# Second group's keys in a buffer of their own, loaded early; sixth and later weight loads held by a one-element write

## The chip, the cores and the metric

The kernel runs on one core of a Trainium2 chip. The metric is the device time of one execution in microseconds (us); lower is better. Five engines work side by side, each with its own instruction stream: TensorE (PE; PEld is its weight load), VectorE (DVE), ScalarE (ACT), GpSimd (POOL) and SyncE (SP, which here only issues DMAs). They wait for each other by semaphores. A DMA issued on SP fetches from main memory into a tile.

## The reference

Three stages, all in float32:

```python
# delta-rule attention: B=4, H=8, S=768, D=48
k_n = k / (norm(k, axis=-1) + 1e-06)
for t in range(S):
    y[:, :, t] = einsum('bhd,bhde->bhe', q[:, :, t], state)
    v_old = einsum('bhde,bhd->bhe', state, k_n[:, :, t])
    state = state + beta[t] * einsum('bhd,bhe->bhde', k_n[:, :, t], v[:, :, t] - v_old)
x = y.transpose(0, 2, 1, 3).reshape(3072, 384)
g = x @ w_gate; x = (silu(g) * (x @ w_val)) @ w_out   # w: 384x1536, 384x1536, 1536x384
h = x @ w_in;   out = elu(h) @ w_out2                 # w: 384x2048, 2048x384
```

## The kernel before

The 3072 tokens are worked in twelve groups of 256: two batches by 128 sequence steps. Group `g` passes through `prepare` (norms of the keys, transposes of queries and keys, Gram matrices, L447 to L604), `invert` (a triangular inverse by 32 small DVE steps, L642 to L724) and `attention` (X, the matrices G, the chain of states, the outputs, their transposes, L746 to L895). Then `moe1(g)` applies the first pair of projections and `w_out` for twelve slices of the hidden width, each with three passes of high and low parts, so that float32 precision comes out of a faster matrix format. Its result goes to memory. After all groups `moe2` does the second pair.

The weights arrive as 64-bit patterns and are decoded on the chip. One weight tile `w0` ... `w17` holds a pair of slices; `load_w` issues its DMAs (L931, L934), and `decode` turns it into high and low parts in about six instructions on ACT (L954, L960, L965, L982) and DVE (L968, L972, L986). Slices `f` = 0, 1 of `moe1` need tiles 0 to 2, slices 2, 3 need 3 to 5, and so on. So the first 130 us hold the attention of groups 0 and 1, the decoding of eighteen tiles and the first slices of `moe1(0)`, all on DVE and ACT.

The order of the instructions on every engine is fixed ahead of the run by a planner (`Order.run`, L134 on): each step names the engines it can run on, estimated costs, a priority, and what it reads and writes, and the planner picks the next one. Where it expects PE to be idle it puts in matmuls whose result nobody reads (`fill`, L1217; `fill2`, L1228). It also keeps count of PE's instructions in blocks of 256 (`fetch`, L104 on).

Names that the change and the prediction touch: `kp` and `qp` are the tiles of keys and queries, shared by all groups; the zero columns of `kp` are set in `c1` (L394). `loads(g, ...)` issues the DMAs of keys, queries and values. `norm` inside `prepare` squares the keys (L477 on DVE or POOL, L481 on ACT), sums (L485), takes the root (L489) and inverts (L493, L495); `nkn` (L536) scales the keys; `rk` (L541) and `kb` (L546) copy them on. The X step is L772 on PE and its copies into `gr` are L777; the G step is L792 in four sets per group, and its copies are L801. `gr` is also written by `kb`, so that POOL's `kb` of group 1 waits until group 0 has read it. `load_w` of tile 5 and later carries `mark[PAUSE]`, the last X copy of group 0, as a predecessor in the planner alone: no semaphore stands behind it.

Of the kernel before, what the change touches and what calls it, by code (L numbers as in the profile page):

```python
# [245 lines left out]
def delta_moe_kernel(ctx: ExitStack, tc: tile.TileContext, q, k, v, beta,  # L246
# [15 lines left out]
    UNTIL = 170e3  # L262
    JOIN = (4,)
    AHEAD = 5
    PAUSE = (0, 'x')
    HOLD = (0, 'm')
    WARM = 8
    P1 = 14.7
# [25 lines left out]
    low = zd[:, 1:2]  # L294
    nbt = T("nbt", [128, NI, B * H])

    kp = T("kp", [128, 16, 64])
    qp = T("qp", [128, 16, 64])
    R = T("R", [128, 16, 96])
    kq = T("kq", [128, 2, 4, 2, 128])  # L300
# [81 lines left out]
    def consts():  # L382
        def c0():
            make_identity(nc, ident)
            G.memset(strict, 1.0)
            for r in range(4):
                s = strict[32 * r:32 * r + 32, :]
                G.affine_select(out=s, in_=s, compare_op=ALU.is_ge, fill=0.0, base=-1,
                                pattern=[[1, 32]], channel_multiplier=-1)
        add(0, [("POOL", 2500.0, 2500.0, 0, c0)], w=["ident", "strict"])  # L390

        def c1():
            V.memset(neg1, -1.0)
            V.memset(kp[:, :, D:64], 0.0)  # L394
            V.memset(qp[:, :, D:64], 0.0)
        add(0, dve(600, c1, 3), w=["neg1", "kpz", "qpz"])

        def c2():
            for r in range(4):
                q0 = slice(32 * r, 32 * r + 32)  # L400
                V.tensor_copy(eye[q0], ident[q0, q0])
            V.tensor_reduce(out=low, in_=ident.rearrange("p (r h m) -> p h r m", r=4, h=2)[:, 1],
                            op=ALU.add, axis=AX.XY)
            V.tensor_scalar(out=zd[:, 0:1], in0=low, scalar1=-1.0, scalar2=1.0,
                            op0=ALU.mult, op1=ALU.add)
        add(20, dve(220, c2, 6), r=["ident"], w=["eye", "zd"])
# [35 lines left out]

    SHIFT = ((0, 0, 128, 0), (4, 0, 64, 64), (4, 64, 128, 0))

    def loads(g, p, then=None, after=()):
        for a0, a1 in ((0, 1), (1, 2)) if g == 0 else ((0, 2),):
            add(p, dma(196608 * (a1 - a0), lambda a0=a0, a1=a1: nc.sync.dma_start(  # L447
                out=kp[:, a0 * 8:a1 * 8, 0:D], in_=src_of(k, g, a0, a1)), 160.0),
                w=[("k", x) for x in range(a0, a1)], after=after)
        if then:  # L450
            then()
        for a0, a1 in ((0, 1), (1, 2)) if g == 0 else ((0, 2),):
            add(p, dma(196608 * (a1 - a0), lambda a0=a0, a1=a1: nc.sync.dma_start(
                out=qp[:, a0 * 8:a1 * 8, 0:D], in_=src_of(q, g, a0, a1)), 160.0),
                w=[("q", x) for x in range(a0, a1)], after=after)
        for a in range(2):
            def rv(a=a):
                x = src_of(v, g, a, a + 1)
                for u0, p0, p1, m0 in SHIFT:
                    nc.sync.dma_start(out=R[p0:p1, a * 8 + u0:a * 8 + u0 + 4, D:2 * D],  # L460
                                      in_=x[m0:m0 + p1 - p0, u0:u0 + 4])
            add(p, [("SP", 1290.0, 0.0, 196608 / 160.0, rv)], w=[("Rv", a)])

    ALLA = [("ain", n) for n in range(4)]

    def prepare(g, p):
        i, b0 = ax_of(g)
        ss, s, r = sm
        sq = ain[:, 0:768].rearrange("p (u d) -> p u d", d=D)
        two = g == 0  # L470

        def norm(u0, u1, keys):
            u = slice(u0, u1)
            n = D * (u1 - u0)

            def square(e):
                return lambda: e.tensor_tensor(out=sq[:, u], in0=kp[:, u, 0:D], in1=kp[:, u, 0:D],  # L477
                                               op=ALU.mult)

            def squared():  # L480
                A.activation(out=sq[:, u], in_=kp[:, u, 0:D], func=ACTF.Square)  # L481
            part = [("sq", x) for x in keys]
            add(p, dve(n, square(V)) + (act(n, squared, False) if two else pool(n, square(G))),
                r=[("k", x) for x in keys] + ([] if u0 else ALLA[:3]), w=part + ([] if u0 else ALLA[:3]))
            add(p, dve(n, lambda: V.tensor_reduce(out=ss[:, u], in_=sq[:, u], op=ALU.add, axis=AX.X)),  # L485
                r=part + ALLA[:3], w=[("ss", x) for x in keys])

            if g < 2:
                add(p, act(u1 - u0, lambda: A.activation(out=r[:, u], in_=ss[:, u], func=ACTF.Sqrt), False),  # L489
                    r=[("ss", x) for x in keys] + ["sqrt"], w=[("sm", x) for x in keys])  # L490

                def over():
                    V.tensor_scalar(out=r[:, u], in0=r[:, u], scalar1=-1.0, scalar2=-1e-6, op0=ALU.mult,  # L493
                                    op1=ALU.add)
                    V.reciprocal(out=s[:, u], in_=r[:, u])  # L495
                add(p, [("DVE", 400.0, 490.0, 0, over)], w=[("sm", x) for x in keys])
                return
            sk = [("sm", x) for x in keys]

            def guess():  # L500
                V.tensor_scalar(out=s.bitcast(I32), in0=ss.bitcast(I32), scalar1=-0.5,
                                scalar2=float(0x5f3759df), op0=ALU.mult, op1=ALU.add)
            add(p, [("DVE", 100.0, 180.0, 0, guess)], r=[("ss", x) for x in keys], w=sk)
            for _ in range(3):
                def newton():
                    V.scalar_tensor_tensor(out=r, in0=s, scalar=-0.5, in1=ss, op0=ALU.mult, op1=ALU.mult)
                    V.tensor_tensor(out=r, in0=r, in1=s, op=ALU.mult)
                    V.scalar_tensor_tensor(out=s, in0=r, scalar=1.5, in1=s, op0=ALU.add, op1=ALU.mult)
                add(p, [("DVE", 430.0, 510.0, 0, newton)], w=sk)

            def over():
                V.tensor_tensor(out=r, in0=ss, in1=s, op=ALU.mult)
                V.tensor_scalar(out=r, in0=r, scalar1=-1.0, scalar2=-1e-6, op0=ALU.mult, op1=ALU.add)
                V.reciprocal(out=s, in_=r)
            add(p, [("DVE", 500.0, 590.0, 0, over)], w=sk)
# [33 lines left out]
        def trans(a, which):  # L549
# [13 lines left out]
            def rest():  # L563
                add(p, act(512, part(A.copy)) + (dve(512, part(V.tensor_copy)) if two else []),
                    r=[h], w=[("kq", a, which)], use=[h])
            return (436, f, ["ident", n + "z", ("qk"[which], a)], h,
                    [("kq", a, which)], rest)
        batch(p, 2, [trans(0, 0), trans(1, 0)], g > 0)
        for a in range(2):
            add(p, dve(384, lambda a=a: nkn(a)), r=[("sm", a)], w=[("k", a)])  # L570
        if two:
            add(p, dve(512, mb), r=["strict", "nbt"], w=zk, need=[hm])
        batch(p, 2, [trans(0, 1), trans(1, 1)], g > 0)
        later = []
        for a in range(2):
            def scaled(a=a, after=()):
                add(p, (dve if two else pool)(384, lambda: kb(a)), r=["nbt", ("k", a)], w=[("grk", a)],
                    wait=GX[a], after=after)
            if not two:
                scaled()  # L580
            else:
                later.append(scaled)
            for n, c in enumerate(SHIFT):
                add(p + 0.9, act(192, lambda a=a, c=c: rk(a, *c), False), r=[("k", a)],
                    w=[("Rk", a, n)])
        for a in range(2):
            l = []
# [330 lines left out]
    opened = {}  # L918

    sent = []  # L920

    def load_w(n, srcs, p, after=()):
        def f():
            if srcs[0][0].dtype == I32:
                buf[n] = TT(f"w{n}", [128, 2, 2 * DM], I32)
            else:
                buf[n] = TT(f"w{n}", [128, 2, DM])
            for j, (src, cols) in enumerate(srcs):
                rv = buf[n][:, j]
                if not cols:  # L930
                    nc.sync.dma_start(out=rv, in_=src)  # L931
                    continue
                rv = rv.rearrange("p (kk f) -> p kk f", kk=KD)
                nc.sync.dma_start(out=rv, in_=src.rearrange("(kk p) f -> p kk f", p=128))  # L934
# [296 lines left out]
    def warm():  # L1231
        fill(WARM)
        od.fill = fill
        od.quick = quick
    loads(0, 0, betas)
    consts()
    add(0, [("ACT", 1400.0, 1500.0, 0, lambda: A.activation(
        out=sm[2][:, 0:1], in_=neg1, func=ACTF.Sqrt, scale=-1.0))], r=["neg1"], w=["sqrt"])
    add(0, act(128, lambda: A.copy(out=identr, in_=ident), False), r=["ident"], w=["identr"])
    add(0, pe(230 * WARM, warm, 1, 2 * WARM), r=["identr"])  # L1240
    beta_rows()
    prepare(0, att_pri(0))
    rows()
    attention(0, att_pri(0) + 1)

    def new_dt():
        buf['dt'] = TT("dt", [128, 2, 2, DM], I32)
    add(0, [("SP", 1.0, 0.0, 0.0, new_dt)], w=[("dt", 0), ("dt", 1)])
    for n in range(NW):
        load_w(n, src1(n), 1 + n, [] if n < AHEAD else [mark[PAUSE], sent[n - 2]])  # L1250
        tag, tk = (("xh1", ["xh1"]), (0, [("dt", 0)]), ("xl1", ["xl1"]), (1, [("dt", 1)]))[
# [1 line left out]
        decode(n, tag, tk, att_pri(0) + 4.8 + 0.02 * n)  # L1253
    for g in range(NB):
        if g:
            loads(g, 100 + 10 * g if g > 1 else PL1, None, [sent[NW - 1]] if g == 2 else [])
            prepare(g, att_pri(g) - 5 if g > 1 else P1)
            attention(g, att_pri(g) + 1 if g > 1 else P1)
        moe1(g, MP + 100 * g)
# [54 lines left out]
```

## Time and profile before

| | us |
|---|---|
| median of 3 runs (1142.50 to 1144.47) | 1144.07 |
| the profiled execution | 1148.89 |
| span of its trace | 1147.2 |
| PE busy in the span | 1116.3 |
| DVE busy | 808.2 |
| ACT busy | 562.0 |

The profiled execution took 1.69 us around its span and 4.82 us more than the median. The rows below are of this one execution; "idle before" in square brackets is the time in which the engine had nothing to run just before the instruction, with what ended it.

### The profile page before, as it was taken

The numbers are of one execution on the slowest core, as the hardware profiler recorded it, in microseconds if no ns is written. First come the engines' busy times: TensorE is split into PE (matmuls) and PEld (weight loads), VectorE is DVE, ScalarE is ACT, GpSimd is POOL, SyncE is SP. The second block draws the span as 40 slices with busy tenths as digits, with TensorE's granted clock in tenths as the row PEclk, the third lists the DMA queues.
The fourth block names the chain that finished last, engine by engine and source line by source line (L and its number), as shares of the span: only waits on it lengthen the run. The fifth ranks groups of instructions, "written<-read, shape, count | busy, mean of one in ns | idle before, by whom it ended". The sixth has DMA issues, their size and how long they took to land.

```text
span 1147.2 us, 34358 instructions
## 1 busy us (share of the span) xinstructions
PE 1116.3 (97%) x14711; PEld 1027.4 (90%) x14711; DVE 808.2 (70%) x2489; ACT 562.0 (49%) x1104; POOL 43.3 (4%) x57
## 2 busy tenths in 40 slices
PE   8899999999999999999999999999999999999998
PEld 6688989999899899899999999988888888898887
DVE  7889877877888777878787775995545444454444
ACT  7798442424343424243424234995545454454444
POOL 0100010100010100000001000000000000000000
PEclk9899999999999999899999899999999999999999
DMA  8770211020202120202020005900101001010000
GB/s 197 212 205 17 44 31 30 16 44 9 51 17 44 25 35 9 51 9 51 9 51 10 22 3 170 344 2 28 55 1 55 1 14 42 1 37 1 28 1 28
DMA packets 107625, 57.36 MB, mean 50 GB/s; under 512 B 77744, under 2 KB 102320, under 8 KB 107472
## 3 DMA queue, kind: packets, MB, share of 16 engines
q1 hardware_dynamic: 107472, 55.16, 18.3%
q8 instruction: 115, 1.88, 0.7%
q14 instruction: 38, 0.31, 0.1%
HBM read 45.71 MB, written 9.44 MB: 48 GB/s over the span
## 4 chain that ended last, share of the span: by engine, by line
PE 86%; DVE 8%; ACT 4%; issue 2%; DVEq 0%; ACTq 0%
PE gv L1028 26%; PE acc L1054 12%; PE acc L1180 9%; PE at L1180 9%; PE gv L1143 9%; PE at L1143 8%; PE at L792 3%; PE at L828 3%; PE at L557 2%; PE at L772 2%; PE at L598 2%; PE at L862 1%; PE acc L1217 1%; DVE sv L834 1%; ACT tb L1035 1%
## 5 line engine op out<-in xcount | busy, mean ns | idle before, releaser
L1028 PE MATMUL gv<-xh,w 128*128 128x256 f32 x1728 | 291.3, 288 | 1.4 <-ACT tb L1035 0.9
L1028 PEld LDWEIGHTS gv<-xh,w 128*128 128x128 f32 x1728 | 241.3, 193 | 7.2 <-ACT tb L1035 2.3
L1054 PE MATMUL acc<-hb,w 128*128 128x256 f32 x1296 | 183.6, 287 | 0.5 <-ACT hb L1042 0.5
L1054 PEld LDWEIGHTS acc<-hb,w 128*128 128x128 f32 x1296 | 165.7, 192 | 6.3 <-issue 2.4
L1035 ACT ACTIVATE tb<-gv 128x256 f32<-128x256 f32 x144 | 55.5, 385 | 226.5 <-PE gv L1028 225.9
L1028 PE MATMUL gv<-xl,w 128*128 128x256 f32 x864 | 151.8, 284 | 2.8 <-issue 2.0
L1028 PEld LDWEIGHTS gv<-xl,w 128*128 128x128 f32 x864 | 125.1, 193 | 3.3 <-issue 2.3
L1038 DVE TENSOR_TENSOR tb<-gv,tb 128x256 f32<-128x256 f32 x144 | 60.3, 419 | 62.2 <-ACT tb L1035 42.9
L1042 ACT CAST hb<-tb 128x256 fp32r<-128x256 f32 x144 | 58.7, 407 | 89.3 <-DVE tb L1038 89.3
L1158 DVE SCALAR_TENSOR_TENSOR hb<-gv,hb 128x512 f32<-128x512 f32 x48 | 33.2, 691 | 92.0 <-ACT hb L1155 92.0
L657 DVE TENSOR_TENSOR ain<-z,ain 128x60 f32<-128x60 f32 (+32 forms) x522 | 89.0, 209 | 2.4
L664 DVE TENSOR_TENSOR z<-z,ain 128x60 f32<-128x60 f32 (+32 forms) x522 | 89.2, 210 | 1.0
L1158 DVE SCALAR_TENSOR_TENSOR hb<-at,hb 128x512 f32<-128x512 f32 x48 | 33.2, 691 | 79.6 <-ACT hb L1155 79.4
L1149 ACT ACTIVATE hb<-gv 128x512 f32<-128x512 f32 x48 | 28.8, 599 | 94.5 <-PE gv L1143 94.3
L1045 DVE TENSOR_TENSOR hb<-tb,hb 128x256 fp32r<-128x256 f32 x144 | 63.2, 439 | 14.4 <-ACT hb L1042 12.8
L1155 ACT ACTIVATE hb<-hb,neg 128x512 f32<-128x512 f32 x96 | 69.7, 726 | 3.0
L1149 ACT ACTIVATE hb<-at 128x512 f32<-128x512 f32 x48 | 28.7, 598 | 78.4 <-PE at L1143 78.1
L1152 ACT ACTIVATE hb<-hb 128x512 f32<-128x512 f32 x96 | 60.9, 634 | 2.9
L792 PE MATMUL at<-gr,R 32*96 32x80 f32 x1480 | 47.9, 255 | 1.5 <-issue 1.5
L792 PEld LDWEIGHTS at<-gr,R 32*96 32x96 f32 x1480 | 39.9, 162 | 8.6 <-issue 2.7
L1143 PE MATMUL gv<-lc,w 128*128 128x512 f32 x144 | 41.2, 394 | 0.0
L1143 PE MATMUL at<-lc,w 128*128 128x512 f32 x144 | 40.9, 394 | 0.0
(212 smaller groups left out, 2080.9 us busy)
## 6 DMA issues: line engine op xcount, KB each, us to landing
w<-in_moe_w_out_dram SPq DMA_DIRECT2D x28, 384.0 KB, 7.1
w<-in_moe_w_in_dram SPq DMA_DIRECT2D x16, 384.0 KB, 6.3
w<-in_moe_w_gate_dram SPq DMA_DIRECT2D x12, 384.0 KB, 8.1
w<-in_moe_w_val_dram SPq DMA_DIRECT2D x12, 384.0 KB, 7.7
qp<-in_q_dram SPq DMA_DIRECT2D x11, 384.0 KB, 6.2
kp<-in_k_dram SPq DMA_DIRECT2D x11, 384.0 KB, 4.6
x2d<-hb SPq DMA_DIRECT2D x12, 256.0 KB, 2.0
R<-in_v_dram SPq DMA_DIRECT2D x24, 96.0 KB, 2.2
```

The source lines that it names most:

```text
L657: V.tensor_tensor(out=t, in0=z[:, l:l + 1, x:y].to_broadcast([128, m, y - x]), in1=an[:, l + 1:32, l:l + 1].to_broadcast([128, m, y - x]), ...
L664: V.tensor_tensor(out=z[:, l + 1:32, x:y], in0=z[:, l + 1:32, x:y], in1=t, op=ALU.add)
L792: PE.matmul(bank[h[c].got[0]][0:96, s * 80:s * 80 + 80], lhsT=R[t, u, :], rhs=gr[t, u, 0:80], start=True, stop=True, skip_group_check=True)
L1028: PE.matmul(dst, lhsT=wt[:, a_, kk * 128:(kk + 1) * 128], rhs=xx[:, kk, :], start=(n == 0), stop=(n == 3 * KD - 1))
L1035: A.activation(out=c['s'], in_=bank[h.got[0]][:, 0:TB], func=ACTF.Silu)
L1045: return lambda: e.tensor_tensor(out=c['h'][:, 1, :], in0=c['s'], in1=c['h'][:, 0, :].bitcast(F32), op=ALU.subtract)
L1054: PE.matmul(o_, lhsT=w[:, a_, d * 128:(d + 1) * 128], rhs=c['h'][:, b_, :], start=(f == 0 and n == 0 and d != 1), stop=(f == F1 - 1 and n ...
L1143: PE.matmul(x, lhsT=W[f][:, 0, a_, kk * 128:(kk + 1) * 128], rhs=x2[n][b_][:, kk, :], start=(m == 0), stop=(m == 3 * KD - 1))
L1152: A.activation(out=c['r'], in_=c['r'], func=ACTF.Exp, scale=-1.0)
L1155: A.activation(out=c['r'], in_=c['r'], func=ACTF.Identity, bias=neg1, scale=1.0)
L1158: V.scalar_tensor_tensor(out=c['r'], in0=bank[h.got[0]], scalar=0.0, in1=c['r'], op0=ALU.max, op1=ALU.add)
L1180: PE.matmul(o, lhsT=c['h'][:, b_, t * 128:(t + 1) * 128], rhs=W[f][:, 1][:, a_, :], start=(f == 0 and m == 0), stop=(f == F2 - 1 and m == 2))
```

## The change

Group 1's keys get a tile of their own, `kpx[1]` (tag `l2`), with its zero columns set on POOL. `loads` is split: `load_k(1)` and `norms(1)` are added to the planner's list ahead of the attention of group 0, the queries and values of group 1 behind it. For group 1 the squares go to a scratch tile `xh0` instead of `ain`, and may be made on DVE or ACT instead of DVE or POOL. `PAUSE` now names a new step, `gate`: it allocates the tile of weight 5 and lets ACT copy one element of `gr`, where X has just been written, into it. The DMAs into that tile must wait for that write, and all DMAs behind them on SP with them.

```diff
-    PAUSE = (0, 'x')
+    PAUSE = 'gate'
...
-    kp = T("kp", [128, 16, 64])
+    kpx = [T("kp", [128, 16, 64]), T("l2", [128, 16, 64])]
...
+        add(0, pool(256, lambda: G.memset(kpx[1][:, :, D:64], 0.0)), w=["l2"])
...
-    def loads(g, p, then=None, after=()):
+    def kkey(g, a):
+        return "l2" if g == 1 else ("k", a)
+
+    def load_k(g, p, after=()):
+        kp = kpx[g == 1]
...
+    def load_qv(g, p, after=()):
...
-    def prepare(g, p):
-        i, b0 = ax_of(g)
+    def norms(g, p):
         ss, s, r = sm
-        sq = ain[:, 0:768].rearrange("p (u d) -> p u d", d=D)
+        kp = kpx[g == 1]
+        sqs = {0: ain[:, 0:768].rearrange("p (u d) -> p u d", d=D)}
+        sk_ = ["xh0"] if g == 1 else ALLA[:3]
...
+            def scratch():
+                if g == 1:
+                    sqs[0] = TT("xh0", [128, 16, D])
+                return sqs[0][:, u]
...
-            add(p, dve(n, square(V)) + (act(n, squared, False) if two else pool(n, square(G))),
+            add(p, dve(n, square(V)) + (act(n, squared, False) if g < 2 else pool(n, square(G))),
...
+    held = set()
...
         def f():
-            if srcs[0][0].dtype == I32:
+            if n in held:
+                held.discard(n)
+            elif srcs[0][0].dtype == I32:
                 buf[n] = TT(f"w{n}", [128, 2, 2 * DM], I32)
...
-    loads(0, 0, betas)
+    load_k(0, 0)
+    betas()
+    load_qv(0, 0)
...
+    norms(0, att_pri(0))
     prepare(0, att_pri(0))
     rows()
+    load_k(1, PL1)
+    norms(1, P1)
     attention(0, att_pri(0) + 1)
+    load_qv(1, PL1)
...
+    def gate():
+        n = AHEAD
+        held.add(n)
+        buf[n] = TT(f"w{n}", [128, 2, 2 * DM], I32) if src1(n)[0][0].dtype == I32 else TT(f"w{n}", [128, 2, DM])
+        A.copy(out=buf[n].bitcast(F32)[0:1, 0, 0:1], in_=gr[0:1, 0, 0:1])
+    mark['gate'] = add(att_pri(0) + 1, act(1, gate, False), r=[("gx", 0, 0)], w=[f"w{AHEAD}", f"w{AHEAD}b"])
...
-            loads(g, 100 + 10 * g if g > 1 else PL1, None, [sent[NW - 1]] if g == 2 else [])
+            if g > 1:
+                load_k(g, 100 + 10 * g, [sent[NW - 1]] if g == 2 else [])
+                norms(g, att_pri(g) - 5)
+                load_qv(g, 100 + 10 * g, [sent[NW - 1]] if g == 2 else [])
```

The planner's order moves with it. On SP, the queue of DMAs, the keys of group 1 stood behind weight 4 and in front of weight 5. Before (the names `w5_20_634` and so on begin with the weight tile's number):

```order
L453 DMA qp_70<-in_q_dram 128x16x48 [waits DMAHW3_49,PE_49]
L934 DMA w4_9_212<-in_moe_w_gate_dram 128x3x256 [waits DMAHW4_49]
L934 DMA w4_9_212<-in_moe_w_val_dram 128x3x256 [waits DMAHW5_49]
L447 DMA kp_69<-in_k_dram 128x16x48 [waits DVE_49,DMAHW6_49,PE_49,Activation_49]
L931 DMA w5_20_634<-in_moe_w_out_dram 128x768 [waits DMAHW7_49]
L931 DMA w5_20_634<-in_moe_w_out_dram 128x768 [waits DMAHW0_49]
```

The same stretch of SP's queue now:

```order
L452 DMA l2_70<-in_k_dram 128x16x48 [waits DMAHW7_49]
L951 DMA w2_7_177<-in_moe_w_out_dram 128x768 [waits DMAHW0_49]
L951 DMA w2_7_177<-in_moe_w_out_dram 128x768 [waits DMAHW1_49]
L954 DMA w3_8_188<-in_moe_w_gate_dram 128x3x256 [waits DMAHW2_49]
L954 DMA w3_8_188<-in_moe_w_val_dram 128x3x256 [waits DMAHW3_49]
L458 DMA qp_71<-in_q_dram 128x16x48 [waits DMAHW4_49,PE_49]
L954 DMA w4_9_233<-in_moe_w_gate_dram 128x3x256 [waits DMAHW5_49]
L954 DMA w4_9_233<-in_moe_w_val_dram 128x3x256 [waits DMAHW6_49]
L951 DMA w5_16_581<-in_moe_w_out_dram 128x768 [waits DMAHW7_49,Activation_49]
```

The keys moved in front of weight 2 and wait for no engine; weight 5 waits for ACT. On ACT, around the second half of the inverse (L724 before, L741 now), the rows before were:

```order
L724 COPY ain_74<-at3_88 128x256
L982 CAST w0_13_525<-xh1_10_289 128x2x384
L982 CAST w1_14_528<-dt_3_138 128x2x384
L954 ACTIVATE w4_9_212<-w4_9_212 128x768
L960 ACTIVATE xh1_15_532<-w4_9_212 128x768
L724 COPY ain_74<-at0_85 128x256
L777 COPY gr_73<-at1_86 128x4x80
```

and they are now:

```order
L741 COPY ain_75<-at3_89 128x256
L501 ACTIVATE sm2_80<-sm0_78 128x16
L1002 CAST w0_14_532<-xh1_10_292 128x2x384
L974 ACTIVATE w4_9_233<-w4_9_233 128x768
L985 ACTIVATE w2_7_177<-w2_7_177 128x768
L741 COPY ain_75<-at0_86 128x256
L1280 COPY w5_16_581<-gr_74 1x1
L577 COPY kq_73<-at3_89 128x4x128
```

The second copy of the inverse now stands behind a sign step (L985); the one-element write follows it, and the transposed keys of group 1 come here instead of some 20 instructions later. On PE, around the second group's inverse, the products of slices 2 and 3 (which read `w5`) stood before it:

```order
L1054 MATMUL acc_84<-hb3_48_1165,w5_35_951 128x256 x9
L1228 MATMUL acc_84<-identr_64 128x256 x12
L1054 MATMUL acc_84<-hb0_52_1222,w5_35_951 128x256 x9
L1228 MATMUL acc_84<-identr_64 128x256 x4
L704 MATMUL at2_87<-ain_74,gr_73 32x32 x32
```

and now stand behind it:

```order
L1248 MATMUL acc_85<-identr_64 128x256 x32
L721 MATMUL at2_88<-ain_75,gr_74 32x32 x32
L721 MATMUL at3_89<-ain_75,gr_74 32x32 x32
L1248 MATMUL acc_85<-identr_64 128x256 x2
L1074 MATMUL acc_85<-hb3_51_1191,w5_39_995 128x256 x9
L1248 MATMUL acc_85<-identr_64 128x256 x4
```

The unread fillers (L1228, now L1248) in front of the inverse's first product grew from 16 to 32.

## Rows read from the trace of the kernel before

**Rows 1.** The page: busy us of each engine, share of the span, instructions.
```profile
PE 1116.3 (97%) x14711; PEld 1027.4 (90%) x14711; DVE 808.2 (70%) x2489; ACT 562.0 (49%) x1104; POOL 43.3 (4%) x57
```

**Rows 2.** Busy us by stretch: PE, PEld, DVE, ACT, POOL, then PE clock, DMA share, GB/s.
```profile
28.00:30.00 2.00, 0.72 (x48) 0.51 (x51) 1.97 (x3) 1.17 (x2) 0.00 (x0) 1.00 0.65 130
32.00:34.00 2.00, 1.01 (x38) 0.72 (x39) 2.00 (x3) 2.00 (x4) 0.40 (x1) 0.50 1.04 375
42.00:44.00 2.00, 2.00 (x46) 1.45 (x47) 1.84 (x4) 0.99 (x5) 0.00 (x0) 0.98 0.47 85
59.40:122.70 63.30, 59.63 (x1244) 55.76 (x1243) 58.86 (x121) 56.29 (x95) 3.55 (x3) 1.00 0.33 89
```

**Rows 3.** Timeline of PE, 28 to 46 us: start, duration, line, tiles, count, idle before.
```profile
29.93 0.39 PE L720 MATMUL at<-z,ain 32*32 32x32 f32 x25 [1.28 <-issue]
32.45 1.01 PE L772 MATMUL at<-gr,ain 32*32 32x80 f32 x38 [0.98 <-ACT ain L724]
35.85 0.76 PE L772 MATMUL at<-gr,ain 32*32 32x80 f32 x26 [2.38 <-issue]
38.05 2.08 PE L1217 MATMUL acc<-identr 128*128 128x512 f32 x4
46.48 0.73 PE L1217 MATMUL acc<-identr 128*128 128x512 f32 x2
```

**Rows 4.** DMA queues in 27.0 to 27.5 us: packets, MB, share of 16 engines.
```profile
q8 instruction: 1, 0.02, 13.8%
```

**Rows 5.** DMA queues in 33.0 to 33.5 us.
```profile
q1 hardware_dynamic: 159, 0.17, 105.1%
q8 instruction: 1, 0.02, 13.9%
```

**Rows 6.** DMA queues in 19.0 to 21.5 us: group 1's queries, 2048 packets in all.
```profile
q1 hardware_dynamic: 2021, 0.51, 121.6%
```

**Rows 7.** Timeline of SP's queue of DMAs (SPq), 27 to 30 us.
```profile
27.65 0.37 SPq L447 DMA_DIRECT2D kp<-in_k_dram  x1
28.07 1.78 SPq L931 DMA_DIRECT2D w<-in_moe_w_out_dram  x2
```

**Rows 8.** Timeline of ACT: a half of group 0's squares, and the stretch at 32 us.
```profile
5.37 0.51 ACT L481 ACTIVATE ain<-kp 128x384 f32<-128x384 f32 x1
32.01 0.39 ACT L724 COPY ain<-at 128x256 f32<-128x256 f32 x1
32.58 1.97 ACT L965 ACTIVATE w<-w 128x768 f16<-128x768 f16 x1
```

**Rows 9.** Timeline of DVE, 37 to 123 us.
```profile
37.41 0.95 DVE L477 TENSOR_TENSOR ain<-kp 128x768 f32<-128x768 f32 x1
41.71 0.49 DVE L801 COPY lc<-at 96x320 f32<-96x320 f32 x1 [1.50 <-PE at L792]
46.07 0.49 DVE L801 COPY w<-gv 96x320 f32<-96x320 f32 x1
47.83 0.74 DVE L840 COPY sv<-at 48x192 f32<-48x192 f32 x2 [0.22 <-PE at L828]
51.11 0.56 DVE L536 TENSOR_TENSOR kp<-kp,sm 128x384 f32<-128x384 f32 x1
122.83 0.56 DVE L895 TENSOR_TENSOR xl<-at,xh 128x384 fp32r<-128x384 f32 x1
```

**Rows 10.** Timeline of PE, 59 to 75 us.
```profile
59.21 0.52 PE L1028 MATMUL gv<-xh,w 128*128 128x256 f32 x3
72.47 1.24 PE L1054 MATMUL acc<-hb,w 128*128 128x256 f32 x9
73.56 1.60 PE L1228 MATMUL acc<-identr 128*128 128x256 f32 x12
```

**Rows 11.** Busy us by stretch as in rows 2, a later group's attention.
```profile
465.00:470.00 5.00, 3.40 (x16) 3.21 (x16) 3.69 (x9) 0.00 (x0) 0.53 (x1) 0.53 0.44 53
```

More of the change, by code (lines that the diff above doesn't have):

```diff
@@ L393, in c1 @@
             V.memset(neg1, -1.0)
-            V.memset(kp[:, :, D:64], 0.0)
+            V.memset(kpx[0][:, :, D:64], 0.0)
             V.memset(qp[:, :, D:64], 0.0)
         add(0, dve(600, c1, 3), w=["neg1", "kpz", "qpz"])
+        add(0, pool(256, lambda: G.memset(kpx[1][:, :, D:64], 0.0)), w=["l2"])
         def c2():
@@ L448, in loads @@
                 out=kp[:, a0 * 8:a1 * 8, 0:D], in_=src_of(k, g, a0, a1)), 160.0),
-                w=[("k", x) for x in range(a0, a1)], after=after)
-        if then:
-            then()
+                w=[kkey(g, x) for x in range(a0, a1)], after=after)
+    def load_qv(g, p, after=()):
         for a0, a1 in ((0, 1), (1, 2)) if g == 0 else ((0, 2),):
@@ L461, in rv @@
                                       in_=x[m0:m0 + p1 - p0, u0:u0 + 4])
-            add(p, [("SP", 1290.0, 0.0, 196608 / 160.0, rv)], w=[("Rv", a)])
+            o = add(p, [("SP", 1290.0, 0.0, 196608 / 160.0, rv)], w=[("Rv", a)])
+            mark.setdefault((g, 'v'), o)
     ALLA = [("ain", n) for n in range(4)]
-    def prepare(g, p):
-        i, b0 = ax_of(g)
+    def norms(g, p):
         ss, s, r = sm
-        sq = ain[:, 0:768].rearrange("p (u d) -> p u d", d=D)
+        kp = kpx[g == 1]
+        sqs = {0: ain[:, 0:768].rearrange("p (u d) -> p u d", d=D)}
+        sk_ = ["xh0"] if g == 1 else ALLA[:3]
         two = g == 0
@@ L474, in norm @@
             n = D * (u1 - u0)
+            def scratch():
+                if g == 1:
+                    sqs[0] = TT("xh0", [128, 16, D])
+                return sqs[0][:, u]
             def square(e):
-                return lambda: e.tensor_tensor(out=sq[:, u], in0=kp[:, u, 0:D], in1=kp[:, u, 0:D],
+                return lambda: e.tensor_tensor(out=scratch(), in0=kp[:, u, 0:D], in1=kp[:, u, 0:D],
                                                op=ALU.mult)
             def squared():
-                A.activation(out=sq[:, u], in_=kp[:, u, 0:D], func=ACTF.Square)
+                A.activation(out=scratch(), in_=kp[:, u, 0:D], func=ACTF.Square)
             part = [("sq", x) for x in keys]
-            add(p, dve(n, square(V)) + (act(n, squared, False) if two else pool(n, square(G))),
-                r=[("k", x) for x in keys] + ([] if u0 else ALLA[:3]), w=part + ([] if u0 else ALLA[:3]))
-            add(p, dve(n, lambda: V.tensor_reduce(out=ss[:, u], in_=sq[:, u], op=ALU.add, axis=AX.X)),
-                r=part + ALLA[:3], w=[("ss", x) for x in keys])
+            add(p, dve(n, square(V)) + (act(n, squared, False) if g < 2 else pool(n, square(G))),
+                r=[kkey(g, x) for x in keys] + ([] if u0 else sk_), w=part + ([] if u0 else sk_))
+            add(p, dve(n, lambda: V.tensor_reduce(out=ss[:, u], in_=sqs[0][:, u], op=ALU.add, axis=AX.X)),
+                r=part + sk_, w=[("ss", x) for x in keys])
             if g < 2:
@@ L520, in prepare @@
             norm(0, 16, (0, 1))
+    def prepare(g, p):
+        i, b0 = ax_of(g)
+        s = sm[1]
+        kp = kpx[g == 1]
+        two = g == 0
         hm = Slots(HB, 1)
@@ L565, in rest @@
                     r=[h], w=[("kq", a, which)], use=[h])
-            return (436, f, ["ident", n + "z", ("qk"[which], a)], h,
+            return (436, f, ["ident", n + "z", kkey(g, a) if which else ("q", a)], h,
                     [("kq", a, which)], rest)
@@ L569, in prepare @@
         for a in range(2):
-            add(p, dve(384, lambda a=a: nkn(a)), r=[("sm", a)], w=[("k", a)])
+            add(p, dve(384, lambda a=a: nkn(a)), r=[("sm", a)], w=[kkey(g, a)])
         if two:
@@ L576, in scaled @@
             def scaled(a=a, after=()):
-                add(p, (dve if two else pool)(384, lambda: kb(a)), r=["nbt", ("k", a)], w=[("grk", a)],
+                add(p, (dve if two else pool)(384, lambda: kb(a)), r=["nbt", kkey(g, a)], w=[("grk", a)],
                     wait=GX[a], after=after)
@@ L583, in prepare @@
             for n, c in enumerate(SHIFT):
-                add(p + 0.9, act(192, lambda a=a, c=c: rk(a, *c), False), r=[("k", a)],
+                add(p + 0.9, act(192, lambda a=a, c=c: rk(a, *c), False), r=[kkey(g, a)],
                     w=[("Rk", a, n)])
```

## The prediction

> **What bounds the kernel now.** I read the page first: PE is busy for 97% of the span and DVE for 70% [rows 1]. PE's useful matmuls are the same before and after, so the time can only change by what PE does besides: idling, unread fillers, and stretches at the lower clock. The table by stretch shows where those are. [...] From 59 to 123 us DVE is busy for 58.86 of 63.30 us, ACT for 56.29 [rows 2]: there the decoding of the weights and the attention of group 1 set the pace, and PE fills. After 123 us PE is the bound almost throughout.
>
> The timeline of PE says what ends its idle time in the first stretch: 1.28 us before row 29.93 and 2.38 us before row 35.85 are put down to "issue", that is to no engine, and 0.98 us before 32.45 to ACT's copy L724 [rows 3]. Both "issue" waits are 128 matmuls apart (25 of L720, 64 + 38 of L772, one filler; the 64 stand in a row between those shown), which with one weight load each is the planner's block of 256 instructions. The DMA view fits that: the queue for instructions, q8, carries one packet of 0.02 MB in 27.0 to 27.5 us [rows 4] and one in 33.0 to 33.5 us [rows 5], about 2.6 us before either wait ends. The first went over a wire with nothing else on it (q8 is the only row); the second shared it with bulk loads that took 105.1% of the engines' time in that half microsecond. If the second was asked for when PE entered the block at 29.93, it took 5.9 us until PE ran on at 35.85. The bulk loads are those that SP issued from 27.65 on: the keys of group 1, then weights 5 and 6 [rows 7].
>
> **The gate and the early keys.** They take those loads away from this stretch. Keys go in front of weight 2, weights 5 and up behind X. What is late next:
>
> First wait (to 29.93 now). The keys lie ahead of weights 2 to 4 now, so weight 4 ends later by what the keys take. Group 1's queries, of the same size and shape, moved 2021 of their 2048 packets in 2.5 us [rows 6], so the keys cost 2.5 us of the wire, and weight 4, which was done before 27 us, may be under way when PE asks for its block. The block then comes later by at most the difference of the two seen: 5.9 us for the one amid bulk loads, and 3.4 us for the other, if that was asked for at about 26.5, when PE was 128 matmuls short of the wait (within L704; an estimate from the counts). So 0 to 2.5 us later; I take 1.0, nearer to the quiet one, since at most the end of weight 4 is in the way.
>
> Second wait (to 35.85). With a quiet wire it ends 3.4 us after the first: 33.3 if the first does not move (29.93 + 3.4), 35.8 if it moves by the full 2.5, 34.3 as taken. It is no longer alone: ACT's second L724 now stands behind a sign step of 1.97 us [rows 8], where it began at 32.01 before. ACT starts L982 when DVE's L972 is done, some 0.9 us later than now since the sum over the squares goes first; with L954 and the sign that puts L724's end at about 33.4. So X's second half ends between 34.4 and 36.5, against 36.6 now (35.85 + 0.76) [rows 3].
>
> From there four G sets with fillers run to DVE's copy at 46.07 [rows 9]. The clock decides their pace: four fillers took 2.08 us at half clock, where two took 0.73 at full [rows 3]. DVE's 1.50 us of idle at 41.71, released by PE's L792 [rows 9], is part of this. From below, DVE itself cannot be at the copy of 46.07 before about 44.0: its instructions from 27.9 on, one after the other, with the same share of slowing down by POOL as now. From above it stays where it is. I take the point where the 1.50 us of idle go: -1.5 (bounds 0 and -2.1).
>
> **Work that changes engine or place.** Up to group 0's last output DVE loses two L536 (0.56 each) and two copies of states to ACT (0.74 for two [rows 9]) in this stretch and gets one decode step of 0.95 (the length of L477, the same 768 elements [rows 9]): 1.86 less, 0.95 more, -0.9. So PE's first L1028 comes at about 56.8 for 59.21 [rows 10].
>
> Behind that DVE has more to do than now until group 1's last output at 122.83 [rows 9]. By the order of both: two more copies of G (0.49 each), two more copies of states (0.74), one more pair around the gate product (0.4 each, taken as 0.8), one decode step in and one sign step out: +2.5. In this stretch DVE idles for 63.30 - 58.86 = 4.4 us now [rows 2]; I let half of the extra work fall into that idle time (bounds: all, none): +1.3. The squares go from DVE (0.95) to ACT (twice 0.51 [rows 8]); on ACT they stand before the first L724, where ACT waited about 1 us for PE, so they cost nothing; if that cover is gone they cost 1.0. The memset of `l2` and the one-element write are hidden likewise: POOL is busy for 4% [rows 1]; the write is one short ACT instruction, 0.2 at most.
>
> At the same point of DVE's order PE has done 9 more matmuls of L1028 than now. At the pace of L1054, of the same shape, 9 take 1.09 us (72.47 to 73.56 [rows 10]): -1.1.
>
> Behind the wait of SP's new gate stand weights 5 to 17 and the values of group 1. The values wait for group 0's G sets anyway; weight 5 is asked for at about 33.5 instead of 28.07 [rows 7]. Its first decode step on ACT comes after five G copies, at about 39, some 5.5 us after the request; that is close to what such loads take, so I cost it at nothing, up to 1 us if it lands late.
>
> Sum: -1.5 - 0.9 + 1.3 - 1.1 = -2.2 us. On the profiled execution that is 1148.89 to 1146.7; on the median, which lies 4.82 us lower, 1144.07 to 1141.9.
>
> [...] The trace has PE waiting 2.38 us with no engine ahead of it, as a packet of the instruction queue moves amid bulk loads [rows 3, 5]. [...]
>
> **The rivals.**
> The clock stays up. If PE's idle stretches shrink so far that the clock never falls, the G sets run at the DVE bound (-2.1) and group 1's extra work falls wholly into idle time (0 instead of +1.3): -2.1 - 0.9 - 1.1 = -4.1, 1140.0. For it: the clock fell in the middle of three waits of 1.28, 0.98 and 2.38 us [rows 3] and one of them goes. Against: PE still waits in 28 to 34 us for the first block and for ACT's L724.
> The wait moves. The first block comes 2.5 us later, the second is back where it was, the clock falls as now: 0 - 0.9 + 1.3 - 1.1 = -0.7, 1143.4. For it: weight 4 is on the wire later. Against: the rows say nothing of what is on the wire at 27 us after the change.
> Nothing to remove. The "issue" waits are not the bulk loads' doing and stay at 1.28 and 2.38 us wherever the loads go; nothing is gained there, and the extra work is not covered: 0 - 0.9 + 2.5 - 1.1 = +0.5, 1144.6. For it: the first wait came with a quiet wire [rows 3, 4]. Against: the second, amid loads, was longer by 1.1 us. [...]
> Weight 5 comes too late: slower. Its last decode step (L986 into `w5`) stood before the inverse of group 1 on DVE and now stands behind it; the products of slices 2 and 3 follow, and PE's fillers before the inverse grow from 16 to 32. Two products are 18 matmuls, 2.2 us, at 1.09 for 9 [rows 10], that are not done while PE waits, and a later wait behind ACT's in-order queue comes on top (1 us). It decides if PE has not caught up at group 1's outputs, so that the 1.1 us there are lost too: -0.7 + 1.1 + 2.2 + 1.0 less the 0.9 us of fillers that shrink later = +2.7, 1146.8. For it: the fillers' count. Against: in the order PE has caught up by then.
>
> Later groups are reordered as well. Such a wait can cost there what it costs here: at 465 to 470 us PE was busy for only 3.40 of 5.00 us, at a clock of 0.53 [rows 11]. Where it will fall after the change the rows can't say; I add 1.5 us on either side.
>
> **How the numbers follow.** Forecast -2.2: 0.41, its own range 1140.4 to 1143.4. Clock stays up: 0.17. The wait moves: 0.18. Nothing to remove: 0.04. Weight 5 too late: 0.20. A measurement of this kernel tells a change from none at about 0.2%, 2.3 us. Below 1141.8 lie all of "clock stays up" and about half of the forecast: faster 0.39. Within 2.3 us lie the other half, "moves" and "nothing": 0.41. Slower: 0.20. The range runs from the best case less 1.0 to the slower case less 0.5: 1139.0 to 1146.3.
>
> **What would show it.** Right: the "issue" wait before the second X batch is under 1.2 us; the clock is back at 1.00 before 40 us; DVE's idle time before its second G copy is under 0.5 us; the first L1028 comes before 57.5 us; group 1's last L895 before 122. Wrong: an "issue" wait of 2 us or more anywhere from 28 to 42 us, or ACT waiting for weight 5's DMA; L1028 before 57.5 but L895 of group 1 after 122.8 would say that the extra DVE work ate the gain.

## The result, and the profile after

| | before | after |
|---|---|---|
| median of the runs | 1144.27 us (6 runs, 1142.5 to 1145.9) | 1153.70 us (6 runs, 1151.0 to 1160.6) |
| profiled execution / its span | 1148.89 / 1147.2 us | 1151.01 / 1149.3 us |

Slower: the ratio is 1.0092, 95% interval 1.0063 to 1.0121. The forecast was 1141.9, its range ended at 1146.3. The two profiled executions differ by only 2.1 us, because that of before took longer than any of its six timed runs and that of after is the shortest of its own; what follows is read from where each stretch loses, and decided by medians.

The new code stands lower in the file: L1028 is now L1048, L720 L737, L772 L789, L598 L615, L801 L818, L895 L912, L1228 L1248. PE's row of the page, against [rows 1]:

```profile
PE 1113.4 (97%) x14732; PEld 1024.8 (89%) x14732; DVE 808.8 (70%) x2493; ACT 561.8 (49%) x1101; POOL 43.5 (4%) x58
```

21 matmuls more. PE's timeline at the start, against [rows 3, 10] (start, duration, line, tiles, count, idle before):

```profile
27.94 0.39 PE L737 MATMUL at<-z,ain 32*32 32x32 f32 x25 [1.76 <-issue]
30.19 1.34 PE L789 MATMUL at<-gr,ain 32*32 32x80 f32 x64 [1.85 <-ACT ain L741]
...
34.59 0.91 PE L789 MATMUL at<-gr,ain 32*32 32x80 f32 x64
...
54.35 0.51 PE L1048 MATMUL gv<-xh,w 128*128 128x256 f32 x3
```

The "issue" wait of 2.38 us before X's second half is gone; that half ends at 35.50. The table by stretch, against [rows 2] (PE, PEld, DVE, ACT, POOL, then PE's clock, DMA share, GB/s):

```profile
28.00:30.00 2.00, 0.34 (x25) 0.22 (x24) 0.00 (x0) 2.00 (x3) 1.05 (x1) 0.96 0.72 244
32.00:34.00 2.00, 1.63 (x6) 1.03 (x4) 2.00 (x4) 1.83 (x3) 0.00 (x0) 0.69 0.00 0
36.00:38.00 2.00, 2.00 (x40) 1.42 (x36) 2.00 (x5) 2.00 (x7) 0.00 (x0) 1.00 0.84 285
54.50:121.80 67.30, 63.05 (x1275) 59.15 (x1274) 62.57 (x133) 55.90 (x91) 3.48 (x3) 1.00 0.32 91
```

The clock is back at 1.00 before 38 us, and the first gate product starts at 54.35 us where it started at 59.21: 4.9 us won. Two rows of DVE, against [rows 9], show how long that lasts:

```profile
43.55 0.47 DVE L818 COPY w<-gv 96x320 f32<-96x320 f32 x1
121.95 0.54 DVE L912 TENSOR_TENSOR xl<-at,xh 128x384 fp32r<-128x384 f32 x1
```

2.5 us ahead at the copy, 4.9 at 54 us, and 0.9 at the end of group 1 (122.83 before). By the end of the span it is 2.1 us behind. The waits view of PE from 57 to 750 us (line, releaser: us in total, times, longest) names the "issue" waits of that stretch:

```profile
PE gv L1048 <- issue: 4.4, 5, 1.6
PE at L615 <- issue: 3.0, 2, 1.6
PE at L789 <- issue: 1.2, 1, 1.2
PE at L809 <- issue: 1.0, 2, 0.6
PE at L879 <- issue: 0.9, 1, 0.9
PE at L845 <- issue: 0.8, 1, 0.8
PE at L574 <- issue: 0.4, 1, 0.4
PE at L903 <- issue: 0.4, 1, 0.4
```

12.1 us in 14 waits. The same view of before sums to 8.5 in 11:

```profile
PE at L598 <- issue: 2.7, 2, 1.9
PE gv L1028 <- issue: 2.5, 3, 1.0
PE at L792 <- issue: 1.5, 4, 0.5
PE at L720 <- issue: 1.0, 1, 1.0
PE at L828 <- issue: 0.8, 1, 0.8
```

Two of the 14 on the timeline:

```profile
153.98 0.34 PE L789 MATMUL at<-gr,ain 32*32 32x80 f32 x8 [1.21 <-issue]
...
352.67 0.31 PE L615 MATMUL at<-kq 48*32 48x64 f32 x5 [1.34 <-issue]
```

and what lies around them in the table by stretch:

```profile
150.30:153.99 3.69, 2.46 (x129) 2.13 (x129) 0.85 (x2) 1.77 (x5) 0.00 (x0) 1.00 0.02 4
353.00:357.00 4.00, 4.00 (x62) 3.78 (x66) 2.61 (x6) 0.38 (x1) 0.52 (x1) 0.64 0.02 4
```

The first stretch runs from one "issue" wait to just past the next: 129 matmuls, a block of 256 instructions and the first of the next, done in 2.5 us, then 1.2 us of nothing. Behind the second wait the clock falls: 0.64 of full speed over 4 us. [rows 11] of before was such a place too: the clock of 0.53 there follows a wait of 1.88 us.

### The profile page after: what moved, and what is told of

Read it like the earlier page. It is cut to its first block, busy times and chain, and to the rows that moved or that the text cites. A ratio compares the mean times of both kernels' runs of the same rounds, so it can differ in the third digit from the quotient of the medians.

```text
span 1149.3 us, 34402 instructions
## 1 busy us (share of the span) xinstructions
PE 1113.4 (97%) x14732; PEld 1024.8 (89%) x14732; DVE 808.8 (70%) x2493; ACT 561.8 (49%) x1101; POOL 43.5 (4%) x58
## 3 DMA queue, kind: packets, MB, share of 16 engines
q8 instruction: 115, 1.88, 0.7%
## 4 chain that ended last, share of the span: by engine, by line
PE 79%; DVE 10%; ACT 4%; DMA 3%; issue 2%; SPq 2%; ACTq 0%; DVEq 0%
PE gv L1048 24%; PE acc L1074 10%; PE acc L1200 9%; PE at L1200 9%; PE gv L1163 9%; PE at L1163 8%; PE at L809 2%; PE at L845 2%; DMA w<-in_moe_w_val_dram 2%; PE at L615 1%; PE at L789 1%; PE at L574 1%; DVE hb L1065 1%; PE at L879 1%; DMA w<-in_moe_w_out_dram 1%
## 5 line engine op out<-in xcount | busy, mean ns | idle before, releaser
L1048 PE MATMUL gv<-xh,w 128*128 128x256 f32 x1728 | 288.5, 287 | 3.5 <-ACT tb L1055 1.6
L1048 PEld LDWEIGHTS gv<-xh,w 128*128 128x128 f32 x1728 | 240.6, 192 | 8.3 <-ACT tb L1055 3.4
L1048 PE MATMUL gv<-xl,w 128*128 128x256 f32 x864 | 152.1, 285 | 4.9 <-issue 3.5
L1048 PEld LDWEIGHTS gv<-xl,w 128*128 128x128 f32 x864 | 125.2, 193 | 6.7 <-issue 4.6
L1065 DVE TENSOR_TENSOR hb<-tb,hb 128x256 fp32r<-128x256 f32 x144 | 64.2, 446 | 14.4 <-ACT hb L1062 13.4
L809 PE MATMUL at<-gr,R 32*96 32x80 f32 x1480 | 45.8, 251 | 1.1 <-issue 1.0
L809 PEld LDWEIGHTS at<-gr,R 32*96 32x96 f32 x1480 | 38.1, 159 | 7.8 <-issue 1.6
L1163 PE MATMUL gv<-R,w 128*128 128x512 f32 x144 | 40.8, 393 | 0.0
```

What stands on the lines that cost most here:

```text
L809: PE.matmul(bank[h[c].got[0]][0:96, s * 80:s * 80 + 80], lhsT=R[t, u, :], rhs=gr[t, u, 0:80], start=True, stop=True, skip_group_check=True)
L1048: PE.matmul(dst, lhsT=wt[:, a_, kk * 128:(kk + 1) * 128], rhs=xx[:, kk, :], start=(n == 0), stop=(n == 3 * KD - 1))
L1065: return lambda: e.tensor_tensor(out=c['h'][:, 1, :], in0=c['s'], in1=c['h'][:, 0, :].bitcast(F32), op=ALU.subtract)
L1163: PE.matmul(x, lhsT=W[f][:, 0, a_, kk * 128:(kk + 1) * 128], rhs=x2[n][b_][:, kk, :], start=(m == 0), stop=(m == 3 * KD - 1))
```

## The experiments

All kernels with a list take the planner's own order up to the first gate product (or to 190 us) and then a list of step numbers read from another kernel's plan:

```diff
+OWN = 272
...
+REST = (
...
+            if total - left >= OWN:
...
+                for at, (i, e_) in enumerate(todo):
...
+                    t = start_of(o, *a[:4])
+                    if t is not None:
+                        pick = (t, o, a)
+                        break
```

`todo` is the list; of its steps the first whose inputs and slots are there is taken. In start_new_rest_old and the kernels made from it L1048 is L1188, L615 L755, L789 L929, L737 L877 and L809 L949.

**Which half of the plan costs.** start_new_rest_old: the list of before behind the start of after.

> The changed kernel up to its first gate product (272 steps), then every engine in the order of the kernel before (a list; fillers as there, block phase of PE's instructions within 3 matmuls). Theory A (the plan made anew for the rest is what costs): the first 57 us keep their gain of 3 to 5 us and nothing is lost later, 1139 to 1142 us, idle PE after 60 us about as before (some 13 us). Theory B (the earlier start itself is paid back, whatever the order, by waits for weights or by the clock): 1149 to 1154 us.

1143.42 us, before measured beside it 1143.61: ratio 0.9998 (0.9983 to 1.0013). That is in neither range: the loss is gone, the gain is not there either.

start_old_rest_new: the other way round.

> The kernel before up to its first gate product (269 steps), then every engine in the order of the changed kernel. Theory A: the old start without the gain, then the new order's loss, 1152 to 1158 us. Theory B: as the kernel before, 1143 to 1146 us.

1157.12 us, ratio 1.0106 (1.0069 to 1.0144). The loss comes with the plan for the rest. Nothing in the buffer, the gate or the early keys makes it.

keys_only undoes the gate, gate_only undoes the keys:

```diff
-    PAUSE = 'gate'
+    PAUSE = (0, 'x')
```

> Second group's keys in their own buffer and asked for with the first weights, weight loads held back as before (no gate). Its order from the second group on is nearly that of the changed kernel. Theory A: the same loss as the changed kernel, 1149 to 1155 us, since the order comes with the keys. Theory B, with the late weight 5 as the cause: the loss goes with the gate, 1142 to 1146 us.

> Weight loads wait for the gate, the second group's keys as before. Theory A: its order is a third one, so its time says what a third plan gives: anything from 1140 to 1154 us, with the loss, if any, spread over later groups. Theory B with weight 5 as the cause: 1149 to 1155 us, the loss already there before 130 us.

1152.34 us, ratio 1.0066 (1.0043 to 1.0090), and 1143.20 us, ratio 0.9996 (0.9979 to 1.0013). The loss goes with the keys, or with the order that comes with them, so the late weight 5 is not its cause.

**Bad luck of a profile, or of a plan.** before_again is the unchanged kernel.

> The kernel before, unchanged, against itself. Ratio 1.000 within 0.002; it gives a second profile of the start: if the first gate product again comes at 61 to 62 us and the low clock again lasts some 10 us between 30 and 42, the start's gain of 4 to 5 us is real; if it comes at 57 to 59, most of that gain was the first profile's bad luck.

Ratio 1.0004 (0.9985 to 1.0023). Its first gate product came at 57.42 us (59.21 in the first profile, not the 61 to 62 of the expectation), so of the 4.9 us some 3 stand against this profile too, and 1.8 belonged to the first one. Over all traces it comes at 52.8 to 55.7 us with the new start (ten) and at 57.3 to 59.8 with the old (four).

priority_14_8:

```diff
-    P1 = 14.7
+    P1 = 14.8
```

> The changed kernel with one number of the planner's other than there: the second group's priority 14.8 instead of 14.7, where the first weights' unpacking has 14.8. The start stays; the plan after some 57 us is another one, and from the second group's end to about 390 us it is step for step that of the kernel before. Theory A (the plan drawn for the rest decides): 1139 to 1145 us. Rival (the change itself costs later, by its buffer, its gate or its earlier start): 1149 to 1155 us.

1150.26 us, ratio 1.0057 (1.0034 to 1.0081). Theory A missed: from 124 to 403 us, a third of PE's useful matmuls (all but fillers and tiny ones), this kernel follows the order of before step for step, and it is still slow. The rival's range held, but the rival does not: start_new_rest_old has the same buffer, gate and start without the loss. Matched by useful matmuls done, its profile is 1.1 us behind that of start_new_rest_old at 423 us and 5.2 us at 711: it loses where its order departs again.

new_to_190_us (list of before from 190 us on):

> The changed kernel in its own order until the second group's results are sent (about 190 us on the chip), the rest in the order of the kernel before. The two profiles with the same start put 3.9 of the 8.4 us that the new order loses before 192 us. Theory A with the loss spread evenly: about half of it, 1146 to 1150 us. If one place in the second group decides alone: 1151 to 1154 us; if it is all later: 1142 to 1145 us.

1154.86 us, ratio 1.0093 (1.0073 to 1.0114): all of the loss, with the order of before after 190 us. That ruled out "the order of the later groups". Matched by useful matmuls, its profile is 1.4 us behind that of start_new_rest_old at the first gate product, 6.4 at 187 us, 11.2 at 307 and 10.5 at the end: some 4 us are lost after 190 us, in one and the same order. What differs from start_new_rest_old there is only what has passed before: its trace holds 14732 matmuls, the other's 14714, so the block boundaries fall 18 matmuls apart in the same work.

new_start_rest_of_gate_only:

> The changed kernel up to its first gate product, the rest in the order of gate_only. In their profiles gate_only's rest was 4 us shorter than that of the kernel before when the low clock is taken out. Theory A, if times of start and rest add up: 1138 to 1141 us. If the waits for PE's instructions move with the block phase and do not add up: 1142 to 1147 us.

1141.76 us, ratio 0.9976 (0.9963 to 0.9990): faster than before.

**Block boundaries.** In every trace the rows behind an "issue" wait stand about a whole number of 128 matmuls apart. The 16 traces hold 212 such waits; the place within 128 slips from 93 early to 62 near 640 us, by one or two per 60 us and nearly alike in all of them (what takes these places is not shown), and all but seven waits, of 0.2 to 0.5 us each, lie on that grid. Of the 205, 203 end 2.1 to 3.3 us after a packet of 16 KB began on q8, the queue for instructions (1.88 MB in 115 packets on the page), 2.6 at the median, which I read as PE waiting for its next block. Over the 16 profiles there are 1379 blocks between 75 and 700 us. Of the 64 that PE went through in under 2.5 us, 50 ended in a wait of about 0.3 us or more (0.94 us on the mean of all 64); of the 185 that took 2.5 to 3.4 us, 65; of the 959 of over 4.5 us, three. So theory P: the place of the boundaries decides. The tests move them and leave the work alone.

old_rest_plus_14_tiny and old_rest_plus_7_tiny change one number in start_new_rest_old (tiny matmuls ahead of the first gate product; QUICK is twice their number):

```diff
-QUICK = 0
+QUICK = 28
```

> start_new_rest_old with 14 tiny 32x16 matmuls (about 0.4 us) put in front of its first gate product, nothing else; every later block boundary of PE's instructions falls 14 matmuls earlier in the work. Theory P (each 128 matmuls that take less than about 3.4 us end in a wait for the next instructions, so the place of the boundaries decides): with the boundaries laid 14 matmuls earlier over the profile of start_new_rest_old, the shortfalls below 3.4 us between 57 and 700 us sum to 18.3 instead of 7.1 us, so some 11 us of waits more, and low clock behind them: 1150 to 1158 us. Rival O (the order of the work decides, boundaries are noise): 1143 to 1145 us.

1144.76 us, ratio 1.0016 (1.0000 to 1.0033). Against theory P. The trace holds 14742 matmuls against 14714, so each tiny one counts twice and the shift was 28, not 14. For that shift, too, the shortfalls (what blocks lack to 3.4 us) spoke for more waits; the view from 57 to 750 us has 8.1 us in 10, where start_new_rest_old has 8.4 in 9. These waits are of one execution of 1139.70 us; what those near the median waited is not shown.

> start_new_rest_old with 7 tiny matmuls (0.2 us) in front of its first gate product. The trace of old_rest_plus_14_tiny holds 28 matmul records more, not 14, so each tiny one takes two places in the instruction stream; this is a shift by 14. Theory P: over the profile of start_new_rest_old the shortfalls below 3.2 us after 75 us go from 4.2 to 14.5 us (9.4 at the shift of 28 that the earlier run had): 5 to 10 us of waits more and low clock behind them, 1148 to 1155 us. Rival O: 1143 to 1145 us. If it stays there again, short blocks alone do not make the waits in this order of work.

1153.59 us, ratio 1.0078 (1.0057 to 1.0099). As theory P had it: seven matmuls of 32x16 in front of unchanged work cost 10 us (9 by the ratios). The waits view, start_new_rest_old first:

```profile
PE gv L1188 <- issue: 3.1, 3, 1.3
PE at L755 <- issue: 3.0, 2, 2.2
PE at L949 <- issue: 1.5, 3, 0.9
PE at L877 <- issue: 0.8, 1, 0.8
```

and with the seven:

```profile
PE gv L1188 <- issue: 7.6, 5, 2.4
PE at L755 <- issue: 5.3, 4, 2.7
PE at L929 <- issue: 2.5, 2, 1.8
```

8.4 us in 9 waits against 18.5 in 16 (the smaller lines of the second left out here). The longest:

```profile
301.78 0.43 PE L755 MATMUL at<-kq 48*32 48x64 f32 x4 [2.66 <-issue]
```

The DMA queues from 298.9 to 299.8 us (packets, MB, share of 16 engines) have its block amid the next group's loads:

```profile
q1 hardware_dynamic: 780, 0.15, 139.5%
q8 instruction: 1, 0.02, 7.7%
```

Its surroundings by stretch, with the loads on the wire and the clock at half behind it:

```profile
296.50:299.20 2.70, 2.62 (x156) 2.31 (x153) 2.10 (x7) 0.58 (x1) 0.00 (x0) 1.00 1.06 179
302.00:306.00 4.00, 4.00 (x22) 3.86 (x18) 2.29 (x5) 0.00 (x0) 0.52 (x1) 0.50 0.03 7
```

After 57 us the clock is at half for 20 us in this profile and for 7 us in that of start_new_rest_old: at half pace up to 7 us lost (an estimate), beside 10 of waits; the spans differ by 14.4. That execution took 1157.00 us, the median is 3.4 lower.

new_less_28_fillers and new_28_fillers_tiny edit the changed kernel where the planner emits 16 pairs of fillers ahead of group 1's inverse; the second also puts 28 tiny ones there:

```diff
-                    self.fill(n)
+                    self.fill(2 if n == 16 else n)
+                    if n == 16:
+                        self.tiny(28)
```

> The changed kernel in its own order, with 28 of the 32 filler matmuls before the second group's inverse left out, so that later boundaries fall 28 matmuls later in the work. Theory P: the shortfalls over the changed kernel's profile go from 11.2 to 3.3 us, so 6 to 8 us less waiting and less low clock behind it: 1141 to 1147 us. Rival O, with fillers that only fill waits: 1152 to 1155 us; with fillers that delay work by their whole 4 us: 1150 us.

1140.64 us, ratio 0.9986 (0.9974 to 0.9998): 13 us under the changed kernel (12 by the ratios) and just under the range of theory P, by leaving out 28 fillers that take 3.4 us. Not because of their time:

```profile
68.15 0.64 PE L1248 MATMUL acc<-identr 128*128 128x256 f32 x4
73.54 1.93 PE L721 MATMUL at<-ain,gr 16*32 16x32 f32 x128 [4.75 <-DVE ain L704]
```

The same place in the changed kernel:

```profile
68.43 4.00 PE L1248 MATMUL acc<-identr 128*128 128x256 f32 x32
73.90 1.28 PE L721 MATMUL at<-ain,gr 16*32 16x32 f32 x126 [1.47 <-DVE ain L704]
```

PE waits for the same step of DVE, longer, and goes on 0.4 us sooner. The gain is in the "issue" waits: 2.7 us in 6 for 12.1 in 14, 9.4 of the 11.7 us between the two spans. Their longest lines:

```profile
PE gv L1048 <- issue: 0.9, 1, 0.9
PE at L615 <- issue: 0.5, 1, 0.5
```

> The changed kernel with the same 28 fillers made tiny (32x16 instead of 128x256), so that their time goes and the boundaries stay. Theory P: 1150 to 1154 us, at most the fillers' 3 to 4 us gained. Rival O as for new_less_28_fillers, 1150 to 1155 us: the two runs together part boundary from filler time.

1159.27 us, ratio 1.0149 (1.0125 to 1.0173). The expectation that the boundaries stay was wrong for the reason above: the trace holds 14760 matmuls, 28 more than the changed kernel, so they move the other way. Between this kernel and new_less_28_fillers lie only 28 tiny matmuls, 0.66 us on the timeline, and 18.6 us of time:

```profile
69.46 0.66 PE L1256 MATMUL acc<-ident 32*32 32x16 f32 x56
```

Its longest lines (they stand two lower in the file):

```profile
PE gv L1050 <- issue: 4.3, 3, 2.0
PE at L617 <- issue: 4.1, 4, 1.7
PE acc L1076 <- issue: 2.9, 2, 2.1
```

13.5 us in 12 waits, and 17 us at half clock after 57 us (7 in either of the two others).

gate_rest_less_12_tiny leaves out tiny matmuls that pad the start of new_start_rest_of_gate_only:

```diff
-                    self.quick(n)
+                    self.quick(n - 24)
```

> new_start_rest_of_gate_only with 12 of the tiny matmuls left out that pad PE's instructions at 22 us, so that all later boundaries fall 12 matmuls later. Theory P: over its profile the shortfalls after 68 us go from 10.4 to 7.1 us, and before 50 us from 7.0 to 7.9 us: 1138 to 1141 us, a version better than both. Rival O: 1141 to 1143 us.

1137.83 us, ratio 0.9955 (0.9934 to 0.9975), 14664 matmuls for 14688: a shift of 24, not the 12 expected. Faster than both kernels, by 5.4 us than before measured beside it. Its waits sum to 3.8 us in 8, those of new_start_rest_of_gate_only to 8.9 in 10.

**What the start is worth.** start_old_rest_new_less_28 leaves out the 28 fillers in start_old_rest_new.

> start_old_rest_new with 28 of its 32 fillers left out as in new_less_28_fillers: the old start with the new order and the good boundaries (3 matmuls from those of new_less_28_fillers). Theory P: the 13 us come back here too, 1140 to 1145 us, and what lies above 1140.6 us is what the change's start is worth: 3 to 4 us if the profiles' gain at 60 us survives to the end, nothing if it is given back. Rival O: 1155 us.

1146.58 us, ratio 1.0017 (1.0003 to 1.0031), 1.6 us above the range of theory P: the 10 us come back with the old start as well. Against new_less_28_fillers the new start is worth 0.0031 of 1144 us, 3.5 us. The other two pairs give 0.2 us (0.9998 against 1) and 1.6 us (1.0106 against 1.0092), each to about 2 us or worse.

| kernel | matmuls | blocks under 2.5 us, 75 to 700 us | "issue" waits, 57 to 750 us | half clock after 57 us | profiled execution | median |
|---|---|---|---|---|---|---|
| new_less_28_fillers | 14704 | 0 | 2.7 us in 6 | 7 us | 1139.30 | 1140.64 |
| changed kernel | 14732 | 6 | 12.1 in 14 | 7 | 1151.01 | 1153.70 |
| new_28_fillers_tiny | 14760 | 7 | 13.5 in 12 | 17 | 1156.54 | 1159.27 |
| start_new_rest_old | 14714 | 1 | 8.4 in 9 | 7 | 1142.61 | 1143.42 |
| old_rest_plus_7_tiny | 14728 | 10 | 18.5 in 16 | 20 | 1157.00 | 1153.59 |
| old_rest_plus_14_tiny | 14742 | 4 | 8.1 in 10 | 3 | 1139.70 | 1144.76 |

Within each half of the table the useful work of the rest is the same, and but for a few swaps of neighbours so is its order.

## Why the prediction was wrong, step by step

*The start.* Right in kind, too small in size. The second "issue" wait went and the clock came back before 40 us. That holds beyond this profile: in none of the ten traces of this start does such a wait stand before X's second half, and in the four of the old start it took 2.4 to 3.3 us. DVE's copy came 2.5 us earlier (-1.5 forecast; -2.1 the bound, which counts on POOL slowing DVE: in the profile of before L968 took 1.81 us at 31.41, beside POOL's L527, and 0.95 us at 34.40, with POOL idle), the first gate product 4.9 us earlier (-2.4 forecast) or 3.1 against the second profile of before. DVE did not idle before its second G copy. The first wait, taken to end 1.0 us later than 29.93, ended at 27.94 here, after 1.76 us, and anywhere from 28.4 to 30.4 in the nine other traces of the same start, after 1.4 to 3.7 us: that wait is as long as ever, and in six of the ten it passes the 2 us that were to count as wrong. In the profile after itself all five signs held, the last one, 121.95 for "before 122", by a hair; that none of the signs of being wrong showed there is partly luck. ACT did not wait for weight 5 (its loads were taken to land some 5.5 us after the request; in the first 60 us of before the ten loads from `moe_w_out` took 3.6 to 9.0 us to land, 7.1 at the median); it waited 1.02 us before 23.00 and 1.75 before 26.45 for weights behind the keys, which the prediction had not priced.

*Group 1.* Forecast +1.3 - 1.1, a loss of 0.2; measured 4.0 between 54 and 122 us. The picture behind the slower rival is in the trace: 32 fillers, then the inverse, still waiting 1.47 us for DVE. With the same start and the old order group 1 ends 2.9 us sooner (119.09 in start_new_rest_old). But neither this nor weight 5 is what made the kernel slower: new_less_28_fillers ends group 1 at 123.46, later than all of them, and takes 1140.64 us; and keys_only, without the gate, lost as much.

*Later groups: the step that failed.* "I add 1.5 us on either side" for "such a wait", of which "where it will fall after the change the rows can't say". It is the term that decided, and it was nearly seven times its size: with the start the same, the new plan costs 10.3 us (1153.70 against 1143.42). Nor did the range carry it on the slow side: its end, 1146.3, lies below the slower rival's 1146.8, where 1.5 more would have put it at 1148.3. Shown is the main cause, the boundaries of PE's instruction blocks: moved, they take the loss out of the new plan (1140.64) and put it into the old one (1153.59). How the 10.3 us divide is less clear. In the two profiles the waits for instructions are 3.7 us more, the fillers of group 1 take 2.2 us more (48 for 30 of them), waits for DVE and ACT 0.4; 2.1 of the 8.4 us between these spans I can't assign. The median lies further off than this profile, and the changed kernel's runs carry a granted clock of 0.996 (1151.0 us) down to 0.991 (1160.6 us): in the longer ones, I infer, more of its waits are followed by low clock. That last link rests on six pairs of clock and time; it is not shown by their traces.

The prediction treated the wait as a bad event of unknown place. Its place is in the profile: blocks of 128 matmuls, their times, and from the order the number of matmuls that the change adds ahead of them. With 21 more, every boundary after group 1 moved: 2 blocks of before between 75 and 700 us took under 2.5 us, 6 of the changed kernel. new_less_28_fillers moved them back, with no such block left, and turned the same plan into one that beats before, just (0.9986, 0.9974 to 0.9998).

*The rival "nothing to remove".* It took the waits to have nothing to do with the loads. The start speaks against it, the rest of the span half for it: the 1.21 us before 153.98 fell on a wire with a DMA share of 0.02, so a short block waits without loads too. Over the 16 profiles the waits went with the length of the block: three of the 959 blocks of over 4.5 us ended in one, and 50 of the 64 under 2.5 us. By where the blocks begin, the waits after 57 us came to 2.7 to 13.5 us in the new plan, 8.1 to 18.5 in the old.

*Open.* Why the shift of 28 in old_rest_plus_14_tiny cost nothing although it has short blocks (in that profile, 5 us under the median, one wait of 3.1 us, one of 1.8, the rest small): the time of the block alone does not fix its wait. And what the start is worth at the end, 0.2 to 3.5 us.

## What to carry to other kernels

When a kernel's PE shows "issue" waits a fixed number of instructions apart, count the instructions that a change adds or takes away ahead of a stretch of small matmuls, and lay the new boundaries over the old profile's times before pricing anything else. A planner that replans everything after an edit makes each edit a draw; to see the edit itself, hold the rest of the order fixed, and then try the same order with a few instructions more or fewer, since the blocks' times alone did not foretell every shift (old_rest_plus_14_tiny). Here that was worth more (13 us) than the edit (0.2 to 3.5).

## What the runs showed of the hardware

A 32x16 matmul of f32 operands took two places in PE's instruction stream here: seven of them made 14 records more (14728 against 14714), 28 made 56 (14760 against 14704). And fillers that hid in a wait were not free of consequences: the 3.4 us of 28 fillers cost at most 0.4 where they stood (PE went on at 73.90 with them, at 73.54 without), their places in the instruction stream cost 13 us by the end.
